# Where four early FFN1 matmuls stand among quad 2's scores, where v of quad 2 is loaded, and where beta is computed

## The chip, the cores and the metric

The kernel runs on one core of a Trainium2 chip. The metric is the device time of one execution in microseconds, from the medians of several runs; lower is better. A core has a matrix engine (TensorE, "PE" in the profile; its weight loads are listed apart as "PEld"), a vector engine (VectorE, "DVE"), a scalar engine (ScalarE, "ACT"), GpSimd ("POOL") and a sync engine ("SP"). Each engine works through its own instructions in the order in which the program lists them, and waits on semaphores for what other engines and transfers (DMAs) must have done. TensorE writes to PSUM, which has eight banks; here a bank holds one 128x448 result in f32.

## The reference

Two stages. First an attention without softmax, for batch 8, 12 heads, 448 positions and head size 64:

```
scores = q @ k^T / 8
attn   = max(scores, 0)^2 / 448
x      = attn @ v                       # (8, 12, 448, 64)
```

Then the heads are put side by side, which gives 3584 rows of 768, and go through a feed-forward layer with a slope per column below zero:

```
h   = x @ w_in                          # w_in: 768 x 2048
g   = max(h, 0) + alpha * min(h, 0)
out = g @ w_out                         # w_out: 2048 x 768
```

Inputs and output are f32; the kernel multiplies in bf16 and accumulates in f32.

## The kernel before

**Tiles.** The twelve heads of a batch are taken four at a time, a "quad": quad n is heads 4g to 4g+3 of batch b, with n = 3b + g, so there are 24 quads. Positions are split into seven chunks of 64. For one chunk j of one quad, `score_mm` (L175) issues four matmuls of 64x64 weights against 448 columns, side by side in the four quarters of the array, and fills a pair of PSUM banks. `relu` (L184 on ScalarE, L186 on VectorE) empties the pair into an `rl` tile, and `square` (L194 on VectorE, L192 on ScalarE) makes the `at` tile from it. When all seven chunks of a quad are squared, `attnv` (L204) issues 28 matmuls, four a chunk, into another pair of banks, and two copies, L214 on ScalarE for the first bank and L215 on VectorE for the second, write one third of xT[b], the transposed input of the feed-forward layer.

**FFN1.** The 2048 columns of h are taken 128 at a time: ff 0 to 15. One ff of one batch is six matmuls (km 0 to 5) of 128x128 weights from `w_in_sb` against 448 columns of xT (`f1_mm`, L238). km 0 and 1 read xT as quad 0 of the batch left it, km 2 and 3 as quad 1 did, km 4 and 5 as quad 2 did. km 2 reads the slice that ScalarE's copy wrote, km 3 the one that VectorE's wrote. `f1_out` takes g from the bank with one instruction on ScalarE (L246) and one on VectorE (L247), which reads `beta_sb` = 1 - alpha. `f2` (L261) does the second product, over the g of two batches.

**Order.** There is no planner: the program is written out by hand in the order in which each engine is to work, and the tile framework adds the waits. Scores of the next quads stand between FFN matmuls, so that TensorE has work while ScalarE and VectorE empty PSUM. `sc(chunks)` issues score matmuls and relus and leaves the squares for later, in the list `late`; `sq(k)` issues the oldest k of them. `ch(n, lo, hi, p)` names chunks lo to hi-1 of quad n, with the relu's engine by the letters of p.

**PSUM.** `take_pair` and `take_bank` hand out the pair or bank that was taken longest ago, in program order. `hold` hands out a bank and keeps it out of the rotation, until a later `take` puts it back. The first matmul into a bank waits for whatever instruction last read that bank.

**The place of the change.** Batch 0's first four FFN1 columns are started before quad 2's A@V is done, as soon as km 0 to 3 can be computed. Their sixteen matmuls are the list `todo` (ff first, km within it), and `some_early(count)` issues the next `count` of them, holding a bank for each new ff. The matmuls km 4 and 5 of these four columns follow at L330, each pair with its `f1_out`, and then quad 3 is transposed (`turn_pe(3)`, L153).

**Transfers.** q, k, v and the weights are loaded and cast by POOL's queue, in program order, one after the other. POOL's transfers go round eight semaphores, so a transfer is issued only when the one eight places ahead of it on that queue has landed. `load_w_in(i)` (L114) loads 512 columns of w_in, ff 4i to 4i+3, in four transfers: km 0, 2 and 4 read two of them, km 1, 3 and 5 the other two. `load_v(n)` (L104) is one transfer. SP's queue carries the first q, alpha, the transposing transfers of later quads, and the output.

Of the kernel before, what the change touches and what calls it, by code (L numbers as in the profile page):

```python
# [13 lines left out]
ALU = mybir.AluOpType  # L14
# [6 lines left out]
def kernel(  # L21
# [10 lines left out]
    nc = tc.nc  # L32
# [27 lines left out]
    alpha_sb = singles.tile([128, KF], F32)  # L60
    beta_sb = singles.tile([128, KF], F32)
# [16 lines left out]
    def hold():  # L78

        i = min(range(8), key=lambda i: (taken[i], i))  # L80
        taken[i] = 10**9
        return i
# [17 lines left out]
    def load_v(n):  # L100
        b, g = divmod(n, NG)
        t = v_pool.tile([128, 2, NJ, D], BF16, tag="v", name="vraw")
        flat = v[b].rearrange("(m two) (pp j) d -> (two pp) m (j d)", two=2, j=NJ)
        nc.gpsimd.dma_start(out=t.rearrange("p m j d -> p m (j d)"), in_=flat[:, 2 * g:2 * g + 2])  # L104
        vraw[n] = t
# [4 lines left out]
    def load_w_in(i):  # L110
        lo, hi = 512 * i, 512 * i + 512
        for hf in range(2):
            for e in range(2):
                nc.gpsimd.dma_start(out=w_in_sb[64 * hf:64 * hf + 64, :, e, lo:hi],  # L114
                                    in_=w_in_v[hf, e, :, :, lo:hi])
# [22 lines left out]
    load_v(0)  # L138
    load_qk(2)
    load_v(1)  # L140
    load_v(2)


    T = {}
# [1 line left out]
    def turn_pe(n, parts=(("q", 0, NJ, "D"), ("k", 0, NJ, "D"))):  # L146
        if n not in T:
            T[n] = T_pool.tile([128, 2, NJ, 128], BF16, tag="T", name="T")
        for name, lo, hi, eng in parts:
            ps = take_bank().bitcast(BF16)  # L150
            for j in range(lo, hi):
                for s in range(2):
                    nc.tensor.transpose(ps[64 * s:64 * s + 64, 128 * j:128 * j + 128], raw[(n, name)][:, s, j], ident)  # L153
            dst = T[n][:, "qk".index(name), lo:hi].rearrange("p j c -> p (j c)")
            copy = nc.vector.tensor_copy if eng == "D" else nc.scalar.copy
            copy(dst, ps[:, 128 * lo:128 * hi])  # L156
# [13 lines left out]
    def score_mm(n, j):  # L170
        ps = take_pair()
        t = T[n]
        for r in range(2):
            for c in range(2):
                nc.tensor.matmul(ps[64 * c:64 * c + 64, r, :S],  # L175
                                 t[64 * r:64 * r + 64, 1, j, 64 * c:64 * c + 64],
                                 t[64 * r:64 * r + 64, 0, :, 64 * c:64 * c + 64],
                                 start=True, stop=True)
        return ps

    def relu(ps, eng):
        rl = rl_pool.tile([128, 2, S], BF16, tag="rl", name="rl")
        if eng == "A":
            nc.scalar.activation(rl, ps[:, :, :S], ACTF.Relu)  # L184
        else:
            nc.vector.tensor_scalar(rl, ps[:, :, :S], 0.0, None, ALU.max)  # L186
        return rl
# [9 lines left out]
    def attnv(n):  # L197
        ps = take_pair()
        vv = vraw.pop(n)
        for j in range(NJ):  # L200
            a = att.pop((n, j))
            for r in range(2):
                for s in range(2):
                    nc.tensor.matmul(ps[64 * s:64 * s + 64, r, :S],  # L204
                                     vv[64 * r:64 * r + 64, s, j, :],
                                     a[64 * r:64 * r + 64, s],
                                     start=(j == 0), stop=(j == NJ - 1))
        b, g = divmod(n, NG)
        if g == 0:
            xT[b] = xT_pool.tile([128, NG, 2, S], BF16, tag="xT", name="xT")  # L210
        if n == 0:
            nc.scalar.activation(xT[b][:, g], ps[:, :, :S], ACTF.Copy, scale=out_scale)
            return
        nc.scalar.activation(xT[b][:, g, 0], ps[:, 0, :S], ACTF.Copy, scale=out_scale)  # L214
        nc.vector.tensor_scalar(xT[b][:, g, 1], ps[:, 1, :S], out_scale, None, ALU.mult)  # L215
# [3 lines left out]
    def sc(chunks):  # L219

        for n, j, eng in chunks:
            late.append((n, j, relu(score_mm(n, j), eng)))

    def sq(k=99, eng="D"):
        for g in late[:k]:
            square(*g, eng)
        del late[:k]
# [8 lines left out]
    def f1_mm(ps, b, ff, ks):  # L236
        for km in ks:
            nc.tensor.matmul(ps, w_in_sb[:, km // 2, km % 2, bass.ts(ff, 128)],  # L238
                             xT[b][:, km // 2, km % 2, :],
                             start=(km == 0), stop=(km == KM - 1))  # L240
# [33 lines left out]
    def ch(n, lo, hi, p=pat):  # L274
        return [(n, j, p[j]) for j in range(lo, hi)]

    load_w_in(0)
    load_w_in(1)
    turn_pe(0, (("q", 0, 4, "D"), ("q", 4, NJ, "A"), ("k", 0, 2, "D"), ("k", 2, FIRST, "D")))
    sc(ch(0, 0, 3))  # L280
# [24 lines left out]
    def some_early(count):  # L305
        for ff, km in todo[:count]:
            if ff not in early:
                early[ff] = hold()
            f1_mm(psum[:, early[ff], :S], 0, ff, (km,))
        del todo[:count]  # L310
# [6 lines left out]
    load_v(5)  # L317
    load_w_out(1)
    todo = [(ff, km) for ff in range(4) for km in range(4)]
    sc(ch(2, 3, 4, "AAAAAAA"))  # L320
    nc.vector.tensor_scalar(beta_sb, alpha_sb, -1.0, 1.0, ALU.mult, ALU.add)
    sq(2)
    sc(ch(2, 4, 7, "AAAAADA"))
    some_early(8)
    square(*late.pop(-2), "A")
    sq()
    attnv(2)
    some_early(8)
    for ff in range(4):
        f1_mm(psum[:, early[ff], :S], 0, ff, range(4, KM))  # L330
        f1_out(psum[:, early[ff], :S], 0, ff)
# [165 lines left out]
```

## Time and profile before

| what | value |
|---|---|
| median of 4 runs | 388.87 us (388.64 to 389.02) |
| the profiled execution, its own time | 388.54 us |
| its span, first to last instruction | 386.8 us |
| TensorE busy | 377.5 us, 98% of the span |
| VectorE, ScalarE, POOL busy | 265.9, 206.4, 63.9 us |
| moved by DMA | 42.97 MB, 111 GB/s over the span |
| granted clock of TensorE | 1.000 |

A row of a timeline gives an instruction's start and length in us, its engine, its line in kernel.py, what it writes and reads, and how many like it follow each other without a pause (x16); in brackets how long the engine was idle before it, and what ended that. Matmuls overlap: one lasts 0.35 us from its start to its result, and the next starts sooner than that. So the distance between starts tells what a matmul costs, not its length, and the row of a group ends when its last result is there. The clock was 1.000 throughout, so durations can be compared over the whole span.

### The profile page before, as it was taken

The numbers are of one execution on the slowest core, as the hardware profiler recorded it, in microseconds if no ns is written. First come the engines' busy times: TensorE is split into PE (matmuls) and PEld (weight loads), VectorE is DVE, ScalarE is ACT, GpSimd is POOL, SyncE is SP. The second block draws the span as 40 slices with busy tenths as digits, with TensorE's granted clock in tenths as the row PEclk, the third lists the DMA queues.
The fourth block names the chain that finished last, engine by engine and source line by source line (L and its number), as shares of the span: only waits on it lengthen the run. The fifth ranks groups of instructions, "written<-read, shape, count | busy, mean of one in ns | idle before, by whom it ended". The sixth has DMA issues, their size and how long they took to land.

```text
span 386.8 us, 7918 instructions
## 1 busy us (share of the span) xinstructions
PE 377.5 (98%) x3228; PEld 210.9 (55%) x3228; DVE 265.9 (69%) x421; ACT 206.4 (53%) x332; POOL 63.9 (17%) x95
## 2 busy tenths in 40 slices
PE   7799999999999999999999999999999999999996
PEld 5444564555665456645555455654555545655554
DVE  4977886776868978789655896689754887626300
ACT  5977686445455664555445554547543475434311
POOL 8567221421022202022110221020000000000000
PEclk9999999999999999999999999999999999999999
DMA  9999999999393775687192871937024300120023
GB/s 159 191 203 204 204 213 218 160 171 189 102 163 65 114 130 80 125 138 119 42 177 51 136 120 42 178 57 135 22 64 105 73 0 23 42 61 2 15 70 81
DMA packets 71365, 42.97 MB, mean 111 GB/s; under 512 B 38432, under 2 KB 71328, under 8 KB 71328
## 3 DMA queue, kind: packets, MB, share of 16 engines
q0 software_dynamic: 26768, 22.45, 39.6%
q1 hardware_dynamic: 44128, 19.65, 24.0%
q8 instruction: 25, 0.41, 0.4%
q10 hardware_dynamic: 432, 0.36, 0.3%
q14 instruction: 12, 0.10, 0.1%
HBM read 45.62 MB, written 11.01 MB: 146 GB/s over the span
## 4 chain that ended last, share of the span: by engine, by line
PE 94%; DVE 2%; ACT 1%; DMA 1%; issue 0%; ACTq 0%
PE psum L238 38%; PE psum L261 38%; PE psum L175 9%; PE psum L204 8%; DVE at L194 1%; DMA qfirst<-in_q_dram 1%; PE psum L153 1%; ACT rl L184 1%; DVE T L156 1%; DVE rl L186 1%; ACT osb L263 0%; DVE qraw L136 0%; ACTq L269 0%; ACT T L156 0%; ACTq L184 0%
## 5 line engine op out<-in xcount | busy, mean ns | idle before, releaser
L261 PE MATMUL psum<-w_out_sb,gT 128*128 128x384 bf16 (+2 forms) x912 | 151.1, 323 | 0.0
L238 PE MATMUL psum<-xT,w_in_sb 128*128 128x448 bf16 x768 | 149.5, 353 | 0.4 <-ACT rl L184 0.4
L261 PEld LDWEIGHTS <-gT 128*128 128x128 bf16 x912 | 86.7, 98 | 63.0 <-issue 8.2
L238 PEld LDWEIGHTS <-w_in_sb 128*128 128x128 bf16 x768 | 73.7, 98 | 72.4 <-issue 5.6
L247 DVE SCALAR_TENSOR_TENSOR gT<-neg,beta_sb,psum 128x448 bf16<-128x448 f32 x128 | 83.2, 676 | 31.1 <-ACT neg L246 31.1
L246 ACT ACTIVATE neg<-psum 128x448 f32<-128x448 f32 x128 | 69.3, 547 | 64.0 <-PE psum L238 62.5
L184 ACT ACTIVATE rl<-psum 128x896 bf16<-128x896 f32 x112 | 97.2, 933 | 0.5 <-PE psum L175 0.5
L194 DVE TENSOR_TENSOR at<-rl 128x896 bf16<-128x896 bf16 x162 | 90.6, 616 | 0.0
L186 DVE TENSOR_SCALAR rl<-psum 128x896 bf16<-128x896 f32 x56 | 60.8, 1086 | 43.2 <-PE psum L175 43.2
L263 ACT COPY osb<-psum 128x384 f32<-128x384 f32 (+2 forms) x57 | 27.0, 474 | 105.3 <-PE psum L261 98.4
L175 PE MATMUL psum<-T 64*64 64x448 bf16 x672 | 45.5, 356 | 3.0 <-DVE T L156 1.1
L97 POOL DMA_DIRECT2D qraw<-in_q_dram x23 | 16.5, 718 | 170.8 <-DVE perm L161 162.6
L204 PE MATMUL psum<-at,vraw 64*64 64x448 bf16 x672 | 37.6, 351 | 0.3 <-DVE at L194 0.2
L204 PEld LDWEIGHTS <-vraw 64*64 64x64 bf16 x672 | 24.3, 106 | 11.0 <-issue 2.8
L175 PEld LDWEIGHTS <-T 64*64 64x64 bf16 x672 | 18.2, 105 | 21.6 <-issue 14.4
L215 DVE TENSOR_SCALAR xT<-psum 128x448 bf16<-128x448 f32 x23 | 14.4, 624 | 16.1 <-PE psum L204 11.7
L97 POOL DMA_DIRECT2D kraw<-in_k_dram x23 | 16.5, 718 | 15.2 <-DMA w_out_sb<-in_moe_w_out_dram 13.3
L104 POOL DMA_DIRECT2D vraw<-in_v_dram x24 | 17.3, 720 | 0.9 <-DMA qraw<-in_q_dram 0.4
L214 ACT ACTIVATE xT<-psum 128x448 bf16<-128x448 f32 x23 | 12.7, 551 | 3.2 <-PE psum L204 3.2
L161 DVE COPY perm<-qraw 128x896 bf16<-128x896 bf16 x18 | 11.0, 610 | 2.1 <-DMA T<-perm 2.1
L114 POOL DMA_DIRECT2D w_in_sb<-in_moe_w_in_dram x16 | 10.1, 629 | 7.4 <-DMA w_in_sb<-in_moe_w_in_dram 2.8
L161 DVE COPY perm<-kraw 128x896 bf16<-128x896 bf16 x18 | 10.9, 607 | 0.0
(24 smaller groups left out, 40.8 us busy)
## 6 DMA issues: line engine op xcount, KB each, us to landing
out_dram<-osb SPq DMA_DIRECT2D x110, 96.0 KB, 2.2
vraw<-in_v_dram POOLq DMA_DIRECT2D x24, 224.0 KB, 7.8
qraw<-in_q_dram POOLq DMA_DIRECT2D x23, 224.0 KB, 4.7
kraw<-in_k_dram POOLq DMA_DIRECT2D x23, 224.0 KB, 6.6
w_in_sb<-in_moe_w_in_dram POOLq DMA_DIRECT2D x16, 192.0 KB, 8.2
w_out_sb<-in_moe_w_out_dram POOLq DMA_DIRECT2D x2, 1536.0 KB, 18.6
qfirst<-in_q_dram SPq DMA_DIRECT2D x1, 448.0 KB, 4.0
T<-perm SPq DMA_TRANSPOSE x18, 6.9
```

What stands on the lines that cost most here:

```text
L97: nc.gpsimd.dma_start(out=t.rearrange("p m j d -> p m (j d)"), in_=flat[:, 2 * g:2 * g + 2])
L161: nc.vector.tensor_copy(p[:, i], raw.pop((n, name)).rearrange("p s j d -> p j s d"))
L175: nc.tensor.matmul(ps[64 * c:64 * c + 64, r, :S], t[64 * r:64 * r + 64, 1, j, 64 * c:64 * c + 64], t[64 * r:64 * r + 64, 0, :, 64 * c:64 * ...
L184: nc.scalar.activation(rl, ps[:, :, :S], ACTF.Relu)
L186: nc.vector.tensor_scalar(rl, ps[:, :, :S], 0.0, None, ALU.max)
L194: nc.vector.tensor_tensor(a, rl, rl, ALU.mult)
L204: nc.tensor.matmul(ps[64 * s:64 * s + 64, r, :S], vv[64 * r:64 * r + 64, s, j, :], a[64 * r:64 * r + 64, s], start=(j == 0), stop=(j == NJ ...
L238: nc.tensor.matmul(ps, w_in_sb[:, km // 2, km % 2, bass.ts(ff, 128)], xT[b][:, km // 2, km % 2, :], start=(km == 0), stop=(km == KM - 1))
L246: nc.scalar.activation(neg, ps, ACTF.Relu, scale=-1.0)
L247: nc.vector.scalar_tensor_tensor(gT[b // 2][:, ff, (b % 2) * S:(b % 2) * S + S], neg, beta_sb[:, ff:ff + 1], ps, ALU.mult, ALU.add)
L261: nc.tensor.matmul(ps, gT[sb][:, ff, bass.ts(c, 128)], w_out_sb[:, hf, ff, lo:hi], start=(ff == 0), stop=(ff == KF - 1))
L263: nc.scalar.copy(o[:, lo:hi], ps)
```

## The change

Four edits:

- `load_v(2)` moves from behind `load_v(1)` to behind `load_w_in(0)`, so w_in's first four transfers are each issued one place earlier on POOL's queue.
- Quad 2's chunk 4 is issued beside chunk 3, and the two squares after it follow both. Four of the sixteen early FFN1 matmuls (column 0, km 0 to 3) now stand between chunks 4 and 5.
- Eight still stand between chunk 6 and quad 2's A@V (now columns 1 and 2), and four stand behind the A@V (column 3), where eight did.
- The instruction that computes `beta_sb` moves on VectorE from ahead of those two squares to behind the second copy of quad 2's A@V.

Since banks are handed out in program order, the banks of chunks 5 and 6, of the four held columns and of what follows change with it. The relus and squares keep their engines and their order.

```diff
     load_qk(2)
     load_v(1)
-    load_v(2)
...
     load_w_in(0)
+    load_v(2)
     load_w_in(1)
...
     todo = [(ff, km) for ff in range(4) for km in range(4)]
-    sc(ch(2, 3, 4, "AAAAAAA"))
-    nc.vector.tensor_scalar(beta_sb, alpha_sb, -1.0, 1.0, ALU.mult, ALU.add)
+    sc(ch(2, 3, 5, "AAAAAAA"))
     sq(2)
-    sc(ch(2, 4, 7, "AAAAADA"))
+    some_early(4)
+    sc(ch(2, 5, 7, "AAAAADA"))
     some_early(8)
     square(*late.pop(-2), "A")
     sq()
     attnv(2)
-    some_early(8)
+    nc.vector.tensor_scalar(beta_sb, alpha_sb, -1.0, 1.0, ALU.mult, ALU.add)
+    some_early(4)
     for ff in range(4):
```

## The prediction

> **What bounds the kernel now.** I read the page's busy row first, then the chain that ended last, then TensorE's instructions in order of time around the edit, and last what ended each of its waits. The profiled execution took 388.54 us (span 386.8), 0.33 under the median of the four runs, 388.87.
>
> ```profile
> PE 377.5 (98%) x3228; PEld 210.9 (55%) x3228; DVE 265.9 (69%) x421; ACT 206.4 (53%) x332; POOL 63.9 (17%) x95
> PE 94%; DVE 2%; ACT 1%; DMA 1%; issue 0%; ACTq 0%
> ```
>
> TensorE (PE) is the bound. A change of order cannot remove matmuls, so it can only fill PE's idle time, and that lies early. The timeline of PE alone:
>
> ```profile
> 19.61 1.34 PE L175 MATMUL psum<-T 64*64 64x448 bf16 x16
> 21.38 1.67 PE L238 MATMUL psum<-xT,w_in_sb 128*128 128x448 bf16 x8 [0.43 <-ACT rl L184]
> 22.98 1.70 PE L204 MATMUL psum<-at,vraw 64*64 64x448 bf16 x28
> 24.61 3.20 PE L238 MATMUL psum<-xT,w_in_sb 128*128 128x448 bf16 x16
> 27.75 0.58 PE L153 MATMUL psum<-ident,qraw 128*64 128x128 bf16 x14
> ```
>
> These are chunks 3 to 6 of quad 2's scores, the first eight FFN1 matmuls, quad 2's A@V, eight more FFN1 matmuls with the eight that finish the four columns, and quad 3's transposes. The four score chunks fill 1.77 us although each needs 0.19: narrow windows show chunk 4 at 19.80, chunk 5 at 20.13, chunk 6 at 20.57, and FFN1 at 21.38. Each start stands 0.05 behind the end of what emptied its PSUM banks:
>
> ```profile
> 19.00 1.09 ACT L184 ACTIVATE rl<-psum 128x896 bf16<-128x896 f32 x1
> 19.83 0.68 ACT L214 ACTIVATE xT<-psum 128x448 bf16<-128x448 f32 x1
> ```
>
> ```profile
> 20.27 1.05 ACT L184 ACTIVATE rl<-psum 128x896 bf16<-128x896 f32 x1
> ```
>
> The relu of (2,2) ends at 20.09 and lets chunk 5 start; the xT copy ends at 20.51, chunk 6; the relu of (2,3) ends at 21.33, FFN1. After 21.38 PE has no wait over 0.15 us up to the end, so what is won here is kept, unless a transfer with a fixed time stops it.
>
> **Prices.** From 24 FFN1 matmuls in one row (41.16, 4.70 long, the last 0.35 of it one matmul), a slot is (4.70 - 0.35)/23 = 0.189. The cost of going between 64-row and 128-row matmuls comes from
>
> ```profile
> 28.65 2.44 PE L238 MATMUL psum<-xT,w_in_sb 128*128 128x448 bf16 x12
> 31.02 0.76 PE L175 MATMUL psum<-T 64*64 64x448 bf16 x12
> 31.72 2.44 PE L238 MATMUL psum<-xT,w_in_sb 128*128 128x448 bf16 x12
> 34.09 0.76 PE L175 MATMUL psum<-T 64*64 64x448 bf16 x12
> ```
>
> Twelve FFN1 take 2.37 to the next start, 12 x 0.189 = 2.27, so 0.10 to go over; three chunks take 0.70 where 0.57 is work, so 0.13 back. After a 64-row group that was itself waited for, the next FFN1 starts 0.31 behind it (A@V's last group at 24.30, FFN1 at 24.61). Density does not hide these 0.23 a round trip: the change adds one.
>
> **The four matmuls between the chunks.** Walking the bank choice with the edit: column 0's held bank is then bank 4, freed by the relu of (2,2) at 20.09, and no longer bank 0, freed at 21.33. Chunks 5 and 6 move to banks 6,7 and 0,1, columns 1, 2, 3 to 5, 2, 3. On PE:
> - Column 0, km 0 starts at 20.13 (where chunk 5 started), km 1 at 20.32. km 2 reads the xT slice ending at 20.51: 20.57; km 3 (VectorE's slice, 20.50): 20.76. Behind them wait chunks 5 and 6, and, through them, their relus.
> - Chunk 5: 20.76 + 0.19 + 0.10 = 21.05, banks free since 20.51. Its relu is third in VectorE's queue, at 21.56 in the profile, some 0.07 sooner without beta ahead; the chunk ends at 21.43, so no delay.
> - Chunk 6 needs the banks that (2,3) leaves at 21.33: 21.38. It ends at 21.76, and its relu began at 21.87 because ScalarE was busy: still in time by 0.1.
> - Eight FFN1 from 21.38 + 0.31 = 21.69 (column 2's bank is free when (2,4)'s relu ends at 22.14, and it is asked for at 22.4), then A@V at 21.69 + 1.51 + 0.10 = 23.30.
> - A@V. In the profile it waits for squares: 1.63 from 22.98 to 24.61, where 7 x 0.189 + 0.13 = 1.46 is work. Its last square (VectorE's three from 22.56 for 1.68) ends at 24.24; the last group is now asked for at about 24.46, so those 0.17 vanish. FFN1 follows at 23.30 + 1.46 = 24.76.
>
> At 24.76 twelve FFN1 are left; in the profile sixteen are left at 24.61. So: 4 x 0.189 = 0.76 off, 0.15 on, 0.61 won; quad 3's transposes start at 27.14. As a check, from the common point 21.38: less 4 slots (0.76), less 0.17 of stall, plus a chunk and its way back (0.31): 0.62.
>
> Bounds of this step: at best the way back costs nothing beyond chunk 6's slot, 0.76 + 0.17 - 0.19 = 0.74 won. At worst the squares are late by as much as A@V is, so the stall of 0.17 stays, and chunk 6's relu slips by 0.1: 0.34 won. I take 0.61, since its prices come from the same pairs of instructions.
>
> **A rule on that switch.** The Trainium skill, TensorEngine Tiling (Array Packing), section Tiling Modes (Key Properties), says that a change of tiling mode, not just of tile, drains TensorE; it gives no time. The rows above show 0.10 and 0.13 where a whole drain would be the matmul's 0.35 less its 0.19 slot, 0.16. At 0.16 each, the 0.12 way back in the check becomes 0.16 and about 0.58 is won. It speaks against splitting FFN1 a second time, but not enough.
>
> **Four matmuls behind A@V instead of eight.** Column 0's km 4 is now fifth behind A@V and no longer ninth. It reads xT of quad 2, ready in the profile 0.64 after FFN1's start (ScalarE 24.71 + 0.55 = 25.26); it is asked for 4 x 0.189 = 0.76 after. Margin 0.1; no cost taken, 0.1 at worst.
>
> **beta.** 0.16 us of VectorE moves behind quad 2's xT copy:
>
> ```profile
> 20.42 0.16 DVE L321 TENSOR_SCALAR beta_sb<-alpha_sb 128x16 f32<-128x16 f32 x1
> 20.49 1.15 DVE L194 TENSOR_TENSOR at<-rl 128x896 bf16<-128x896 bf16 x2
> ```
>
> The squares start 0.07 sooner, which no one on PE waits for any more. At its new place VectorE is idle for 1.9 us until the first FFN1 eviction needs beta. Zero; at worst the 0.07 stands for nothing.
>
> **v of quad 2 behind w_in's first four DMAs**, on POOL's queue alone; SP's and ScalarE's issues are untouched. The fourth is
>
> ```profile
> 10.59 0.63 POOL L114 DMA_DIRECT2D w_in_sb<-in_moe_w_in_dram  x1 [0.65 <-DMA vraw<-in_v_dram]
> ```
>
> ```profile
> DMA to landing us min/median/max: 9.5/9.5/9.5
> ```
>
> so it lands at 20.1. POOL's transfers land in issue order here, 1.0 to 1.8 apart; v of quad 2 lands at 15.4. After the swap w_in's four land one place sooner, the last at about 19.1, and v at about 20.1. Column 0 asks at 20.13 and 20.32 and A@V for v at 23.30: margins 1.2 and 3.2. Even with no place won, 20.1 would do, so zero on both sides. POOL issues as many transfers as before; those behind keep their places and semaphores.
>
> **Sum:** 388.54 - 0.61 = 387.93 on the profiled execution, and 0.33 more on the median: **388.26 us**, 0.16% under. By the bounds 388.1 to 388.6.
>
> **Rivals.**
> - *More than 0.2% (0.78 us) won*, about 388.0 (the best bound, 0.74, and half of the 0.19 by which the four runs scatter either way). For it: what the swapped transfers do to the work ahead of 20 us is not priced. Against: chunk 6 is pinned to 21.38 by ScalarE, and everything behind is counted.
> - *A later transfer takes the gain back.* The transfers run at a share of 1.24 of the engines' time up to 45 us, so their times do not move with PE. Quad 4's k lands at 28.91 + 7.6 = 36.5, its transposes start at 37.58, then 36.97: 0.45 left. w_out's first half lands at 29.67 + 14.5 = 44.2, first used at 45.69, then 45.08: 0.9 left. A landing later by 0.45 starts to cost, by 1.1 leaves nothing: 388.87.
> - *Slower: w_in lands after column 0 asks for it.* Now chunks 5 and 6 stand behind that wait in PE's queue. Chunk 6 has 0.13 of slack; beyond it each microsecond is lost. If w_in's fourth lands at 21.05, nothing is won, and from 21.8, 2.7 after my estimate, the kernel is over 0.2% slower: 389.7. Against it: the landings' even spacing.
> - *The change does not do what it says:* column 0's bank is not free at 20.09 but at 21.33. Then four FFN1, two chunks, eight FFN1 and A@V run from 21.38: 21.38 + 0.76 + 0.10 + 0.38 + 0.13 + 1.51 + 0.10 + 1.46 = 25.82 with twelve left, 0.45 lost, 389.3. The walk of the banks speaks against it.
>
> **How the numbers follow.** 0.2% is about what a measurement of this kernel can tell from no change. The forecast's mechanism has 0.78; since its gain lies only 0.17 under that bound and the runs scatter by 0.19 either way, I give 0.33 of it to faster and 0.45 to the same. Larger gain 0.08; gain taken back 0.03; late w_in 0.08, of which 0.07 slower; bank not free 0.03, half of it slower by scatter. With rounding: faster 0.41, same 0.48, slower 0.11. The range reaches from the larger gain with scatter, 387.7, to no gain at all, 388.9. Its upper end leaves the slower cases out.
>
> **What would show it.** In the changed profile: four L238 matmuls near 20.13 between two groups of L175, with a short wait inside; chunk 6 near 21.38 on ScalarE's relu; A@V near 23.30 lasting 1.46; FFN1 at 24.76; transposes at 27.14; the span near 386.2. Wrong would be a PE wait on w_in_sb or vraw, a start of column 0 at 21.38, or a new PE wait on kraw or w_out_sb behind 27 us.

## The result, and the profile after

Measured side by side, the changed kernel takes 388.01 us (median of 42 runs) and the kernel before 388.64 (60 runs). The ratio is 0.9985, with a 95% interval of 0.9981 to 0.9990: 0.63 us, or 0.15%, less. The forecast was 0.61 less. The times of both kernels fall into two groups some 0.4 us apart, so the median of ten or eleven runs moves with the share of each group; the last section says where they come from.

TensorE alone in order of time, the changed kernel (its lines stand one lower than before: L174 scores, L237 FFN1, L203 A@V, L152 transposes):

```profile
20.02 0.57 PE L174 MATMUL psum<-T 64*64 64x448 bf16 x8
20.55 0.98 PE L237 MATMUL psum<-xT,w_in_sb 128*128 128x448 bf16 x4
21.45 0.72 PE L174 MATMUL psum<-T 64*64 64x448 bf16 x8
22.11 1.69 PE L237 MATMUL psum<-xT,w_in_sb 128*128 128x448 bf16 x8
23.73 1.52 PE L203 MATMUL psum<-at,vraw 64*64 64x448 bf16 x28
25.18 2.44 PE L237 MATMUL psum<-xT,w_in_sb 128*128 128x448 bf16 x12
27.55 0.58 PE L152 MATMUL psum<-ident,qraw 128*64 128x128 bf16 x14
```

Everything in this profile lies 0.41 us later than before already at chunk 3 of quad 2 (20.02 against 19.61), ahead of the first place that the change touches on TensorE. That is why the span shrank by only 0.2 (386.8 to 386.6) where the medians differ by 0.63; the last section says where the 0.41 comes from. So I read the stage from chunk 3 to quad 3's transposes: 27.75 - 19.61 = 8.14 us before, 27.55 - 20.02 = 7.53 changed, 0.61 less. From those transposes to the end of the span it is 359.02 us in both profiles. Nothing was given back behind the stage.

VectorE's last three squares for A@V end at 22.96 + 1.68 = 24.64, and A@V's last group of four matmuls starts at 24.89, so TensorE no longer waits for them and 0.25 is to spare:

```profile
22.96 1.68 DVE L193 TENSOR_TENSOR at<-rl 128x896 bf16<-128x896 bf16 x3
```

The chain of what ended last has hardly moved: PE's share is 94% as before, and TensorE is busy for 98% of the span, as before.

```profile
PE 94%; DVE 3%; DMA 1%; ACT 0%; ACTq 0%; issue 0%
```

### The profile page after: what moved, and what is told of

The parts are those of the page before. It is cut to its first block, busy times and chain, and to the rows that moved or that the text cites. A ratio compares the mean times of both kernels' runs of the same rounds, so it can differ in the third digit from the quotient of the medians.

```text
span 386.6 us, 7917 instructions
## 1 busy us (share of the span) xinstructions
PE 378.5 (98%) x3228; PEld 211.5 (55%) x3228; DVE 266.1 (69%) x421; ACT 206.4 (53%) x332; POOL 64.0 (17%) x95
## 4 chain that ended last, share of the span: by engine, by line
PE 94%; DVE 3%; DMA 1%; ACT 0%; ACTq 0%; issue 0%
PE psum L237 38%; PE psum L260 38%; PE psum L174 9%; PE psum L203 8%; DVE at L193 2%; PE psum L152 1%; DMA qfirst<-in_q_dram 1%; DVE T L155 1%; DVE rl L185 1%; ACT osb L262 0%; DVE qraw L136 0%; ACTq L268 0%; ACTq L262 0%
## 5 line engine op out<-in xcount | busy, mean ns | idle before, releaser
L260 PE MATMUL psum<-w_out_sb,gT 128*128 128x384 bf16 (+2 forms) x912 | 151.1, 323 | 0.0
L237 PE MATMUL psum<-xT,w_in_sb 128*128 128x448 bf16 x768 | 149.8, 353 | 0.0
L260 PEld LDWEIGHTS <-gT 128*128 128x128 bf16 x912 | 86.7, 98 | 63.0 <-issue 8.2
L237 PEld LDWEIGHTS <-w_in_sb 128*128 128x128 bf16 x768 | 73.6, 98 | 72.3 <-issue 5.8
L174 PE MATMUL psum<-T 64*64 64x448 bf16 x672 | 45.5, 356 | 2.8 <-DVE T L155 1.3
L203 PE MATMUL psum<-at,vraw 64*64 64x448 bf16 x672 | 37.4, 351 | 0.2 <-DVE at L193 0.2
L203 PEld LDWEIGHTS <-vraw 64*64 64x64 bf16 x672 | 24.1, 106 | 10.8 <-issue 2.9
L174 PEld LDWEIGHTS <-T 64*64 64x64 bf16 x672 | 18.1, 106 | 21.5 <-issue 14.4
```

The costliest lines, as they stand in the source:

```text
L174: nc.tensor.matmul(ps[64 * c:64 * c + 64, r, :S], t[64 * r:64 * r + 64, 1, j, 64 * c:64 * c + 64], t[64 * r:64 * r + 64, 0, :, 64 * c:64 * ...
L203: nc.tensor.matmul(ps[64 * s:64 * s + 64, r, :S], vv[64 * r:64 * r + 64, s, j, :], a[64 * r:64 * r + 64, s], start=(j == 0), stop=(j == NJ ...
L260: nc.tensor.matmul(ps, gT[sb][:, ff, bass.ts(c, 128)], w_out_sb[:, hf, ff, lo:hi], start=(ff == 0), stop=(ff == KF - 1))
```

## Experiments: one part at a time

"The stage" below is always the distance from chunk 3 of quad 2 to quad 3's transposes, read from TensorE's rows; it does not depend on when an execution got going.

**The order of the matmuls alone.**

```diff
     load_v(1)
+    load_v(2)
...
     load_w_in(0)
-    load_v(2)
...
     sc(ch(2, 3, 5, "AAAAAAA"))
+    nc.vector.tensor_scalar(beta_sb, alpha_sb, -1.0, 1.0, ALU.mult, ALU.add)
     sq(2)
...
     attnv(2)
-    nc.vector.tensor_scalar(beta_sb, alpha_sb, -1.0, 1.0, ALU.mult, ALU.add)
```

(against the changed kernel)

> The changed kernel with v of quad 2 and beta back in their old places: only the order of the FFN1 matmuls differs from before. Measure in the trace, beside the time: from chunk 3 of quad 2 to quad 3's transposes, 8.14 us before and 7.53 us changed. Theory (the four matmuls between the chunks are the whole gain): w_in's fourth transfer lands near 20.1 against column 0 asking for it at 20.1 to 20.3, so no wait or one under 0.1: 7.53 to 7.65, time 0.5 to 0.6 under the kernel before. Rival (w_in has to come sooner, so the move of v is what makes the split work): a wait on w_in of several tenths ahead of column 0, 7.9 or more, time within 0.25 of the kernel before.

Stage 7.54 us (20.05 to 27.59); 388.26 against 388.60 us, ratio 0.9990 (0.9981 to 0.9998). The median is 0.34 under before and not the 0.5 to 0.6 that was expected, because eight of the eleven runs fall into the upper group of times; group by group it lies 0.5 and 0.65 under. Column 0 starts 0.53 behind chunk 3, as in the changed kernel, and without a wait:

```profile
20.05 0.57 PE L175 MATMUL psum<-T 64*64 64x448 bf16 x8
20.58 0.97 PE L238 MATMUL psum<-xT,w_in_sb 128*128 128x448 bf16 x4
```

So 0.60 of the 0.61 is the order of the matmuls, with the banks that follow from it. The move of v was not needed for it: w_in's fourth transfer landed at 20.02, and column 0's second matmul, which needs it, started at 20.77. In an execution that gets going 0.4 sooner the matmul would come near 20.33, still behind the landing.

**v alone, and beta alone**, each on the kernel before.

```diff
     load_v(1)
-    load_v(2)
...
     load_w_in(0)
+    load_v(2)
```

> The kernel before with only v of quad 2 moved behind w_in's first four transfers. Theory: nobody waits for either, so 8.14 us from chunk 3 to quad 3's transposes and the time of before to 0.1. Rival (the swapped transfers pay by themselves): 0.3 or more sooner.

Stage 8.14 (19.64 to 27.77), 388.92 against 388.60, ratio 1.0003 (0.9994 to 1.0011): nothing. (Six of the eleven runs fall into the upper group; in each group the difference to before is under 0.1.)

```diff
-    nc.vector.tensor_scalar(beta_sb, alpha_sb, -1.0, 1.0, ALU.mult, ALU.add)
     sq(2)
...
     attnv(2)
+    nc.vector.tensor_scalar(beta_sb, alpha_sb, -1.0, 1.0, ALU.mult, ALU.add)
```

> The kernel before with only beta moved behind quad 2's A@V. Theory: in the order of before the last square ends A@V's wait and stands behind beta on VectorE, so the squares come 0.07 to 0.09 sooner and A@V ends as much sooner: 8.06 us from chunk 3 to quad 3's transposes, time 0.07 under before, too little for the time alone to tell. Rival (the chain is not VectorE's): 8.14.

Stage 8.06 (19.63 to 27.69), 0.08 less; 388.51 against 388.60, too close for the time to tell. TensorE's rows show where the 0.08 lies. A@V takes 1.54 to the next start where it took 1.63:

```profile
23.02 1.60 PE L204 MATMUL psum<-at,vraw 64*64 64x448 bf16 x28
24.56 3.20 PE L238 MATMUL psum<-xT,w_in_sb 128*128 128x448 bf16 x16
```

beta did hold the squares up, and A@V did wait for them. In the changed kernel A@V asks later and waits for nothing, so there the 0.08 is not added.

**The bank that column 0 is held in.**

```diff
     sq(2)
+    early[0], taken[0] = 0, 10**9
     some_early(4)
```

> The changed kernel with column 0 held in bank 0, which chunk 3 of quad 2 filled last, in place of bank 4; chunks 5 and 6 go back to the pairs of before. The order on every engine is that of the changed kernel. Theory (the gain needs a bank that is free at 20.1): column 0 starts at 21.38 on the relu of (2,3), chunks 5 and 6 behind it near 22.2 and 22.45, A@V near 24.35, and from chunk 3 to quad 3's transposes it takes 8.14 + 0.45 = 8.59 us; time 0.45 over before, 1.06 over the changed kernel. Rival (PE's order alone makes the gain): 7.53 us and 0.6 under before.

Stage 8.56; 389.01 against 388.57 us, ratio 1.0012 (1.0002 to 1.0022). The four matmuls wait 1.19 us for the relu of (2,3), and chunks 5 and 6 stand behind them:

```profile
20.02 0.57 PE L174 MATMUL psum<-T 64*64 64x448 bf16 x8
21.78 0.92 PE L237 MATMUL psum<-xT,w_in_sb 128*128 128x448 bf16 x4 [1.19 <-ACT rl L183]
22.63 0.57 PE L174 MATMUL psum<-T 64*64 64x448 bf16 x8
```

TensorE's order is the same as in the changed kernel. The edit also puts chunks 5 and 6 and A@V into other banks, but the wait that the rows show is column 0's. With the wrong bank the edit costs 0.42 of the stage, with the right one it wins 0.61.

**w_in later.**

```diff
-    def load_w_in(i):
+    def load_w_in(i, hfs=range(2)):
...
-        for hf in range(2):
+        for hf in hfs:
...
+    load_v(2)
+    load_w_in(1, (0,))
     load_w_in(0)
-    load_v(2)
-    load_w_in(1)
+    load_w_in(1, (1,))
```

(`load_w_in(1, (0,))` issues two of its four transfers, `load_w_in(1, (1,))` the other two.)

> The changed kernel with w_in's first four transfers behind v of quad 2 and two transfers of w_in's next columns, so that they land three places later than in the changed kernel. Theory (PE's queue is blocked by the first weight load that has not landed, and chunks 5 and 6 with their relus stand behind it): the fourth lands near 22.0, column 0's km 1 starts near 22.1 where it was 20.32, less 0.13 of slack ahead of chunk 6: 1.6 us lost to the changed kernel, 9.1 us from chunk 3 to quad 3's transposes, time 1.0 over before. Rival (weight loads run ahead and the wait is mostly hidden): under 0.5 lost.

Stage 8.35, so 0.82 lost to the changed kernel, and 0.22 worse than before; 388.95 against 388.57 us, ratio 1.0016 (1.0001 to 1.0030). Two of its ten runs, 390.71 and 390.99, lie well above the rest; why is not shown.

```profile
20.54 0.35 PE L237 MATMUL psum<-xT,w_in_sb 128*128 128x448 bf16 x1 [0.15 <-DMA w_in_sb<-in_moe_w_in_dram]
21.57 0.73 PE L237 MATMUL psum<-xT,w_in_sb 128*128 128x448 bf16 x3 [0.68 <-DMA w_in_sb<-in_moe_w_in_dram]
22.22 0.57 PE L174 MATMUL psum<-T 64*64 64x448 bf16 x8
```

The mechanism is the expected one: the second matmul waits for its weights, and both chunks stand behind it. Counted from chunk 3, the second matmul starts 1.04 later than in the changed kernel, chunk 5 0.98 and chunk 6 0.85. The size, 1.6, was too large. I had spaced the landings by before's 1.0 to 1.8 us; here the transfers of w_in landed about 1.0 apart, and the fourth came at 21.4 instead of 22.0. The rival that weight loads hide most of it (under 0.5) fails too.

**Eight between the chunks.**

```diff
-    some_early(4)
+    some_early(8)
     sc(ch(2, 5, 7, "AAAAADA"))
-    some_early(8)
+    some_early(4)
```

> The changed kernel with eight early FFN1 matmuls between chunks 4 and 5 and four behind chunk 6. The number of matmuls and of changes between 64 and 128 rows is that of the changed kernel. Theory (relus and squares of chunks 5 and 6 become the limit): chunk 5 starts near 21.8 and its relu near 22.2 in place of 21.5, VectorE's three squares end near 24.9, A@V waits for the last, FFN1 follows at 25.26: 0.5 of the 0.61 is given back, 8.03 us from chunk 3 to quad 3's transposes, time 0.1 under before. Rival (only PE's idle time counts, and eight fill it as well as four): 7.53 us or less.

Stage 8.11; 388.54 against 388.57 us, ratio 0.9998 (0.9989 to 1.0007): practically the whole gain is gone, with as many matmuls and as many changes between 64-row and 128-row matmuls. A@V first waits 0.20 for its pair of PSUM banks, which chunk 5's relu on VectorE empties, and then lasts 1.92 from its start to the next, where 1.45 is work. What ends last is its wait for VectorE's last square, which is done at 25.32:

```profile
20.47 1.73 PE L237 MATMUL psum<-xT,w_in_sb 128*128 128x448 bf16 x8
22.13 0.57 PE L174 MATMUL psum<-T 64*64 64x448 bf16 x8
22.64 0.93 PE L237 MATMUL psum<-xT,w_in_sb 128*128 128x448 bf16 x4
23.77 1.99 PE L203 MATMUL psum<-at,vraw 64*64 64x448 bf16 x28 [0.20 <-DVE rl L185]
25.69 2.44 PE L237 MATMUL psum<-xT,w_in_sb 128*128 128x448 bf16 x12
```

TensorE's idle time was only moved: chunks 5 and 6 feed the relus and squares that A@V needs, and those now come late.

**Five between the chunks**, four and eight being known.

```diff
-    some_early(4)
+    some_early(5)
     sc(ch(2, 5, 7, "AAAAADA"))
-    some_early(8)
+    some_early(7)
```

> The changed kernel with five early FFN1 matmuls between chunks 4 and 5 and seven behind chunk 6, in place of four and eight. Theory (chunk 6 is pinned to the relu of (2,3), so 0.13 us ahead of it is still free): chunk 6 starts 0.07 later, one slot of 0.19 is saved behind it: 0.1 more won, 7.42 us from chunk 3 to quad 3's transposes; but chunk 5 is then 0.16 later than VectorE could take it, and the last square comes within 0.05 of A@V's last group. Rival (the squares are already as late as A@V bears): A@V grows by 0.1 or more over 1.45 and the sum stays at 7.53 or over.

Stage 7.55, time 388.24 against 388.60 us, ratio 0.9987 (0.9978 to 0.9996): no better than four. The rival held. A@V starts 0.15 sooner behind chunk 3 than in the changed kernel and lasts 1.62 to the next start instead of 1.45; VectorE stood still for 0.15 ahead of chunk 5's relu, and its three squares follow behind:

```profile
22.29 1.09 DVE L185 TENSOR_SCALAR rl<-psum 128x896 bf16<-128x896 f32 x1 [0.15 <-issue]
23.30 1.68 DVE L193 TENSOR_TENSOR at<-rl 128x896 bf16<-128x896 bf16 x3
```

**Five, with the relus and squares dealt out anew** (against the run with five).

```diff
     some_early(5)
-    sc(ch(2, 5, 7, "AAAAADA"))
+    sc([(2, 5, "A")])
+    sq(1)
+    sc([(2, 6, "D")])
     some_early(7)
-    square(*late.pop(-2), "A")
+    square(*late.pop(0), "A")
```

> Five early FFN1 matmuls between chunks 4 and 5, as in the run before this one that won nothing because A@V waited for the last square, and now ScalarE takes the relu of chunk 5 and the square of chunk 4, VectorE the square of chunk 3 ahead of the relu of chunk 6, and the squares of chunks 5 and 6. Theory (the squares of five matmuls came too late because VectorE's queue stood still until chunk 5 was done): VectorE's last square ends 0.16 sooner, A@V lasts 1.45 again, 7.39 us from chunk 3 to quad 3's transposes (7.53 changed, 7.55 with five), time 0.75 under the kernel before; the step from the changed kernel is too small for the time alone. Rival (ScalarE is then late instead): 7.5 or more.

Stage 7.37; 387.90 against 388.63 us, ratio 0.9980 (0.9972 to 0.9989). A@V is back to 1.45:

```profile
23.18 1.52 PE L203 MATMUL psum<-at,vraw 64*64 64x448 bf16 x28
24.63 2.44 PE L237 MATMUL psum<-xT,w_in_sb 128*128 128x448 bf16 x12
```

It beats the kernel before. Against the changed kernel, 388.22 in the same comparison, the step of 0.16 is shown by the rows; the time alone would not tell it.

**The price of a way between 64 and 128 rows.**

```diff
-            if not last and ff in (6, 12):
-                run(some(3))
+            if not last and ff in (5, 6, 7, 11, 12, 13):
+                run([c[:2] + ("ADA"[(ff + 1) % 3],) for c in some(1)])
```

> The changed kernel with each of the ten groups of three score chunks that stand in the FFN1 of batches 2 to 6 taken apart, one chunk ahead of each of three FFN1 columns: twenty more ways there and back between 128-row and 64-row matmuls, with no other work added, in a stretch where PE has no idle time. Theory (a way there and back costs the 0.23 us of the prediction's rows): 20 x 0.23 = 4.6 us more than the changed kernel, 392.6. By the Trainium skill's rule of a whole drain, priced at 0.16 each way, 20 x 0.33 = 6.5 us, 394.5. Rival (the change of tiling is hidden by the matmuls in flight): under 1 us, 389.0.

392.86 against 388.57 us, ratio 1.0108 (1.0093 to 1.0123). From quad 3's transposes to the end of the span it takes 4.53 us more than in the changed kernel, without a wait of TensorE in that stretch, which is 0.227 for each of the twenty ways there and back (from 128-row to 64-row matmuls and back again). The rows read 0.23; waiting out the rest of a matmul both times would have been 0.33 by the same rows.

```profile
133.43 1.31 PE L237 MATMUL psum<-xT,w_in_sb 128*128 128x448 bf16 x6
134.67 0.38 PE L174 MATMUL psum<-T 64*64 64x448 bf16 x4
134.98 1.31 PE L237 MATMUL psum<-xT,w_in_sb 128*128 128x448 bf16 x6
```

From 133.43 to 134.98 is 1.55 us: seven slots of 0.189 are 1.32, and 0.23 is the way there and back.

## Experiments: what lies outside the stage

**The changed kernel once more.**

> The changed kernel itself, once more, beside the kernel before on the same chip. In the runs so far both kernels' times fall into two groups about 0.4 us apart, and in the two profiles the first 36 matmuls, on the same data, last 3.51 us (before) and 4.02 us (changed). Theory (the moment at which TensorE leaves its slow start differs from execution to execution, whatever the kernel): the two groups appear again in both kernels, the lower groups 0.6 apart and the upper groups 0.6 apart, and the distance from chunk 3 to quad 3's transposes is 7.53 us whichever start the profile shows. Rival (the late start belongs to the changed kernel): one group only in the changed kernel's times, the upper.

388.22 against 388.63 us, ratio 0.9989 (0.9980 to 0.9998). The stage is 7.53 again (19.62 to 27.15), and chunk 3 is where it was before the change. Both groups of times are there: of its own eleven runs, three lie at 387.85 to 387.95, five at 388.17 to 388.42, and three higher, at 388.51 to 388.69. Over all the runs of the first comparison, the changed kernel has 22 of 42 runs up to 388.01, with a median of 387.92, and 19 more from 388.09 to 388.44, median 388.27. The kernel before has 34 of 60 up to 388.69, median 388.50, and 26 from 388.78, median 388.90. (One run of the changed kernel, 390.18, stands in neither group; why is not shown.) The groups are 0.58 and 0.63 apart between the kernels. The rival is out.

But this profile's span is 386.9, with nothing gained on before, and the cause is elsewhere. Below, the wait of VectorE on a transposing transfer, in the kernel before, then in the first and in the second profile of the changed kernel:

```profile
DVE perm L161 <- DMA T<-perm: 2.1, 1, 2.1
```

```profile
DVE perm L160 <- DMA T<-perm: 2.5, 1, 2.5
```

```profile
76.43 0.62 DVE L160 COPY perm<-qraw 128x896 bf16<-128x896 bf16 x1 [4.22 <-DMA T<-perm]
77.49 4.81 DVE L246 SCALAR_TENSOR_TENSOR gT<-neg,beta_sb,psum 128x448 bf16<-128x448 f32 x8
```

In that second profile the transfer landed 1.3 us later than in the first. VectorE is held by it with eight evictions of FFN1 queued behind. The last is done at 77.49 + 4.81 = 82.30, and the second product (L260) has come to its last matmul by then:

```profile
79.26 2.85 PE L260 MATMUL psum<-w_out_sb,gT 128*128 128x384 bf16 x15
82.36 0.34 PE L260 MATMUL psum<-w_out_sb,gT 128*128 128x384 bf16 x1 [0.25 <-DVE gT L246]
```

Counting the shorter wait one matmul earlier, TensorE loses 0.7 us here: from quad 3's transposes to the end it is 359.72 us, not 359.02. Before the change the last eviction ended at 81.32, and its matmul came at 82.30: 0.98 to spare, and as much in the first profile of the changed kernel.

That the change brought this about is not shown, and the rows speak against it. The transfer is issued 40.5 us behind quad 3's transposes in all three profiles (at 68.29, 68.10 and 67.69), so it moves with the stage, and what is to spare is the same in both kernels. With the landing of the second profile, 8.62 behind the issue, the kernel before would lose some 0.6 by an estimate from these rows: 68.29 + 8.62 + the 5.99 from landing to last eviction is 82.90, against its matmul at 82.30. Its 21 runs beside these show no such time (388.45 to 389.03), so whether it is ever hit is open.

**A third perm buffer.**

```diff
-    perm_pool = ctx.enter_context(tc.tile_pool(name="perm", bufs=2))
+    perm_pool = ctx.enter_context(tc.tile_pool(name="perm", bufs=3))
```

> The changed kernel with three perm buffers in place of two: VectorE's copies for the third transposing transfer need not wait until the first has landed. In the changed kernel's second profile that landing came 1.3 us later than in its first (76.31 against 74.99), VectorE stood still for 4.2 us, the last of batch 1's g was ready 0.6 after the second product asked for it, and TensorE lost 0.68 us near 81.4. Theory (this wait takes the gain back in some executions): VectorE no longer waits on the transposing transfer, g is ready a microsecond or more sooner against its use, and the time keeps its lower group at 387.9 and loses only its highest runs: 388.0 to 388.2. Rival (the earlier loads crowd the transposing transfers): TensorE waits for T or the median rises over 388.3.

387.91 us (387.85 to 388.33) against 388.86, ratio 0.9981 (0.9972 to 0.9989). VectorE's wait on the transfer is gone, and it now waits for ScalarE between evictions, the last of which starts at 80.04 and ends at 80.72, for a matmul near 81.7:

```profile
80.04 0.68 DVE L246 SCALAR_TENSOR_TENSOR gT<-neg,beta_sb,psum 128x448 bf16<-128x448 f32 x1 [0.46 <-ACT neg L245]
```

That leaves 0.98 to spare, no more than with two buffers when the transfer lands in time: the last eviction then follows ScalarE, and what the third buffer takes away is the dependence on the landing. The highest times of the run before this one (388.51 to 388.69) do not occur in its eleven. That fits, but the run with five and the new deal (387.70 to 388.26, two buffers) has none either; with one profile of the loss, how often it strikes is not shown.

**The third buffer with five and the new deal** (both edits above).

> The same third perm buffer with five early matmuls and the rebalanced relus and squares. Theory (both effects add): 7.37 us from chunk 3 to quad 3's transposes, no wait of VectorE on a transposing transfer, 387.8 to 388.0, 0.7 or more under the kernel before. Rival (the buffer brings a new wait): over 388.0.

388.11 us against 388.86, ratio 0.9980 (0.9971 to 0.9989); stage 7.37, and no wait on the transfer. The median missed the 387.8 to 388.0 that was expected and meets the rival's number (over 388.0), but the rows show no new wait of TensorE. The two effects stand side by side in the rows, but the median does not tell this version from the two before it: 7 of its 11 runs fall into the upper group, where 4 of 11 did with the buffer alone. Its lowest run, 387.71, is that of the rebalanced version, 387.70.

## Why the prediction was right, point by point

- **What bounds it.** The gain came out of TensorE's idle time in this stage, and what was won stayed: 359.02 us from quad 3's transposes to the end in both profiles.
- **The four matmuls between the chunks.** With 0.41 taken off for the later start, column 0 began at 20.13 (forecast 20.13), chunk 5 at 21.04 (21.05), chunk 6 at 21.38 (21.38), FFN1 at 21.70 (21.69), A@V at 23.31 (23.30), FFN1 at 24.76 (24.76), the transposes at 27.14 (27.14). Bank 4 was what made it; in bank 0 the same order loses 0.42, where the forecast's rival of the bank that is not free had 0.45.
- **The 0.17 of A@V's wait** is gone, as forecast, with a margin of 0.25 that five matmuls use up.
- **A rule on the switch.** The row's 0.23 there and back was right over twenty of them (0.227). The Trainium skill, TensorEngine Tiling (Array Packing), Tiling Modes (Key Properties), says that a change of mode drains TensorE. The runs agree in that every change costs time; priced as the 0.16 that a matmul's row has left behind its slot, an estimate, the twenty would have cost 6.5 us, and they cost 4.53.
- **beta and v at nothing.** Right in the changed kernel. beta alone is worth 0.08 where A@V still waits for the squares. A small step was off: chunk 5's relu began 0.03 sooner without beta and not 0.07, because VectorE then waited for chunk 5 (the relu began 0.11 behind chunk 5's last result, as in the runs with five and with eight); nothing on TensorE depended on it. w_in's fourth transfer landed at 19.13 (forecast 19.1) and v of quad 2 at 20.30 (20.1).
- **Four behind A@V:** no wait of TensorE in the changed profile between FFN1 and the transposes.
- **Late w_in.** The forecast's line, no gain if the fourth transfer lands at 21.05, can be tried on the run with w_in behind: there it landed at 21.4, or 21.2 on the clock of the profile before, and 0.22 was lost to before, where the line gives 0.17.
- **The rival of a later transfer** named two candidates, quad 4's k and w_out, and TensorE waited for neither. What took the gain back in one execution is another transfer, the transposing one near 75 us, which VectorE waits for; I had counted waits of TensorE alone. Nor is it the rival's mechanism, a transfer with a fixed time: this one is issued behind VectorE's work and moves with the stage. It struck in one of the two profiles of the changed kernel, and not in the median.
- **The absolute time** came out 0.25 under the forecast, because three of the four runs shown (388.87) lay in their kernel's upper group; the 60 runs have 388.64. The difference, 0.63 against 0.61, is what the steps were about. The span of 386.2 that the forecast named was 386.6 in the profile, for the 0.41 of the later start; the runs of the lower group have 386.1 to 386.2.
- **The chances** that the forecast lists one by one add up to 0.41, 0.505 and 0.085, where it states 0.41, 0.48 and 0.11. Nothing else rests on them.

## What to carry to other kernels

When TensorE waits between groups of matmuls for PSUM to be emptied, the work put into the gap needs a bank of its own that is free at that moment; walk the bank choice in program order before moving an instruction. Fill the gap only as far as the next consumer allows: four matmuls won 0.61 us, five as much, eight nothing, since the chunks pushed back fed the next wait, and only dealing the relus and squares out anew made five pay. Where a gain is below the scatter of whole runs, measure a stage between two instructions of the same engine.

## What was not expected of the hardware

**The start differs from execution to execution.** The first 36 matmuls on TensorE, the same in all kernels, in the kernel before and in the changed one:

```profile
1.36 3.51 PE L133 MATMUL psum<-ident 128*128 128x128 bf16 x36 [1.36 <-POOL ident masks.py:199]
5.43 0.58 PE L153 MATMUL psum<-ident,qraw 128*64 128x128 bf16 x14 [0.56 <-DVE qraw L136]
```

```profile
1.36 4.02 PE L133 MATMUL psum<-ident 128*128 128x128 bf16 x36 [1.36 <-POOL ident masks.py:199]
5.44 0.96 PE L152 MATMUL psum<-ident,qraw 128*64 128x128 bf16 x14
```

They take 3.51 us in one and 4.02 in the other, and the fourteen transposes behind them 0.58 and 0.96. In the kernel before the starts of the 36 stand 0.107 us apart (the first two 0.08) up to 4.2 us, and 0.056 from there on, which is where the trace's clock record first has the full clock. In the changed kernel's profile they stand 0.107 apart to the last, and the full clock is first recorded at 6.6 us. So the 1.000 in the table ahead of the prediction is not true of the first 4 us, where nothing was compared. Behind this start the second profile is 0.41 later. The mean granted clock over the span is 1.000 and 0.999. It is not the kernel's doing: the second profile of the changed kernel has 4.02 for the warm-up but only 0.59 for the transposes, the full clock at 5.5 us, and chunk 3 at 19.62. The Trainium skill, TensorE: Matmul & The Clock Gate, Part 1 (What's actually happening), says that the array runs at half its clock until a window of activity has passed, and that this window runs freely and does not start with the kernel, so that the moment of the change varies from run to run. The rows agree, in the factor (0.107 to 0.056) and in that the moment varies. It varies more than the half microsecond either way that the section gives: from 4.2 to 7.3 us in the fourteen profiles here.

The two groups of times, 0.35 to 0.4 us apart in both kernels, go with these two starts. In five profiles the full clock came by 4.5 us; chunk 3 started at 19.61 to 19.64, and the profiled execution lies in the lower group of its kernel. In seven it came at 6.2 us or later; chunk 3 started at 19.95 to 20.18, and the execution lies in the upper group. Between them stand the second profile of the changed kernel, which lost its 0.7 us elsewhere, and the one with w_in late (5.9 us, 19.82). The clock of the single runs says the same: of the changed kernel's 22 runs in the lower group 19 have a mean of 1.000, of the 19 in the upper group 18 have less.

**A transposing transfer's landing can slip by more than a microsecond.** Issued near 68 us in each, the first one landed at 74.8, 75.0 and 76.3 us in three profiles, 6.5, 6.9 and 8.6 behind its issue; in the eleven other profiles it was 6.6 to 7.1. VectorE, which waits for it, passes that on to TensorE only when some 1.0 us of slack is used up.
